# The opening of an attention and token-mixer block: c loaded as eight rows and spread by selector products, the gate's load moved behind the weights

## The chip, the cores and the metric

The kernel runs on one core of one Trainium2 chip. The metric is the device time of one execution in microseconds; lower is better. Of the core's engines, PE (TensorE) multiplies, DVE (VectorE), ACT (ScalarE) and POOL (GpSimd) work on elements, and SP (SyncE) issues the transfers. Each engine runs its own instructions strictly in order and waits on semaphores for the others.

## The reference, cut to what matters

The block takes x of 2048 tokens by 1024 channels and a condition c of 1024 numbers. Its first half is an attention over four segments of 512 tokens with a memory between the segments; its second half mixes tokens with a two-layer network.

```python
mod = (_silu(c) @ w_mod).reshape(c.shape[0], 6, 1, -1)
sa, ca, ga, sb, cb, gb = (mod[:, 0], mod[:, 1], mod[:, 2], mod[:, 3], mod[:, 4], mod[:, 5])
h = _layernorm(x, axis=-1) * (1 + ca) + sa
x = x + ga * _A_ref(h, A_wq, A_wk, A_wv, A_wo, A_beta)
...
g = _sigmoid(beta).reshape(1, H, 1, 1)
o = g * a_mem + (1.0 - g) * a_dot
```

So every element of h needs two modulation vectors, sa and ca, and these need silu(c) times a 1024 by 2048 part of w_mod. The gate g, one number for each of 32 heads, weighs the memory against the attention.

## The kernel before, in words

Nothing may start on PE before h exists. The opening therefore does the following.

- The 4 KB vector c is loaded as csb, 128 partitions by 8 (line 98). ACT and DVE make silu(c) from it (lines 99 to 103); DVE copies it out to bc, 128 by 8 by 128 (line 262); PE transposes bc in eight pieces (line 266) and ACT copies the result to scb (line 267): now every partition holds all 1024 values.
- Four tiles of x (128 tokens by 1024) are loaded (line 198). DVE takes their statistics (BN_STATS and BN_AGGR, lines 212 and 213, and a few short instructions on mvs, lines 217 to 220), ACT normalises them (line 222).
- For each of eight chunks of 128 channels two tiles wm of w_mod are loaded (line 284). DVE multiplies each by scb and sums along the row into one column of saca (line 285); line 288 adds 1.
- PE transposes a chunk of the four x tiles (hps, line 227), ACT evicts it with scale and bias from saca (line 229), and the result is split into a high and a low half (lines 113 and 116) as a page h. Weights are loaded raw (rawv, rawq, line 144) and split in the same way into wv and wq.
- PE then projects: nps are keys and values (line 182), qps queries (line 190), for heads of group 0 and group 1. A projection takes high by high first and then the products with the low halves, which DVE or POOL make.
- Segment 1 follows with x tiles 4 to 7 in the same way.

The gate is loaded by one transfer that reads beta for all 128 partitions (line 300), made on ACT and DVE (lines 301 to 304), and multiplied on POOL into bdg, one pair of instructions for each of eight groups (lines 318 and 321). bdg is first needed where DVE multiplies the first memory update up into MZ (line 429), the gate itself by the first values product (line 505).

In the attention, sx, sy and sz (line 445) are scores for the row maxima, which DVE reduces (line 446); a (lines 469 to 476) are scores again, whose exponentials p ACT writes, POOL selects (line 480) and splits into ph (line 484), which PE multiplies by the values (pv, line 498).

No engine's order is written by hand. A planner (class Order) records the program, gives each instruction a modelled duration and runs it forward and backward a few times; set_order then fixes the order of PE, DVE, ACT, POOL and SP. A load whose source is read again for every partition (a partition step of 0) is modelled with an added latency, DMA_SPREAD, of 7000 ns. The planner sees the whole program, so a change of the opening may change the order everywhere behind it.

Of the kernel before, what the change touches and what calls it, by code (L numbers as in the profile page):

```python
# [9 lines left out]
F32 = mybir.dt.float32  # L10
# [4 lines left out]
ALU = mybir.AluOpType  # L15
# [29 lines left out]
def attention_and_mlp(ctx, tc, x, wq, wkv, wo, beta, w1, b1, w2, b2, c, wm_a, wm_b, out):  # L45
# [25 lines left out]
    top = top_pool.__enter__()  # L71
    edge.tile([P, 8], F32, name="pad")
    acst.tile([P, 8], F32, name="pad2")
    psum = ctx.enter_context(tc.tile_pool(name="psum", bufs=1, space=PSUM))
# [22 lines left out]
    csb = acst.tile([P, 2, NK], F32, name="csb")  # L97
    SY.dma_start(csb[:, 0], c)
    A.activation(csb[:, 1], csb[:, 0], AF.Exp, scale=-1.0)
    V.tensor_scalar_add(csb[:, 1], csb[:, 1], 1.0)  # L100
    V.reciprocal(csb[:, 1], csb[:, 1])
    sc = const.tile([P, NK], F32, name="sc")
    V.tensor_mul(sc, csb[:, 0], csb[:, 1])

    saca = acst.tile([P, NK, 2], F32, name="saca")
# [154 lines left out]
    xs = {0: [load_x(s1p, tt) for tt in range(4)]}  # L260
    bc = s1p.tile([P, NK, P], F32, name="bc")
    V.tensor_copy(bc, sc.unsqueeze(2).to_broadcast([P, NK, P]))
    for i in range(2):
        ps = bank("pj", 2, f"scps{i}")
        for j in range(4):
            T.transpose(ps[:, 128 * j:128 * j + 128], bc[:, 4 * i + j], ident)
        A.copy(scb[:, 512 * i:512 * i + 512], ps)
# [25 lines left out]
    for g in range(2):  # L293
        first_chunk(g, NK - 1)
    xs[1] = [load_x(s2p, tt) for tt in range(4, 8)]
    norm_tiles(s2p, xs[1])
    for ct in range(NK):
        h_chunk(s2p, xs[1], 1, ct)
    gate = top.tile([P, 3, H], F32, name="gate")
# [4 lines left out]
    V.tensor_scalar(gate[:, 1], gate[:, 0], -1.0, 1.0, op0=ALU.mult, op1=ALU.add)  # L304

    left.__exit__(None, None, None)
# [651 lines left out]
HOLD = 1000.0  # L958
EARLY = 60000.0
STAY = 3000.0  # L960
SLACK = 1.06
# [17 lines left out]
def size_of(a):  # L979
    return math.prod(s[1] for s in a.ap) * mybir.dt.size(a.dtype)  # L980
# [51 lines left out]
def cost(x):  # L1032
# [20 lines left out]
    if e == "DVE":  # L1053
        if op == "ISA":
            return 135 + 1.05 * n, 220 + 1.05 * n, False
        if op == "TensorTensor":
            d = 145 + 1.055 * n
        elif op == "TensorScalarPtr":
            d = 190 if n < 64 else 120 + 1.1 * n
        else:  # L1060
            d = {"TensorCopy": 820, "BNStats": 680, "TensorReduce": 554}.get(op, 195)
# [16 lines left out]
class Order:  # L1078
# [155 lines left out]
    def side(x):  # L1234
# [26 lines left out]
    def forward(self, key):  # L1261
        n, E = len(self.X), self.E
        key = [-1e18 if i in self.follows else k for i, k in enumerate(key)]
        strong, weak, open_ = [[] for _ in range(n)], [[] for _ in range(n)], [0] * n
# [7 lines left out]
        ready, start, fin, seq = [0.0] * n, [0.0] * n, [0.0] * n, []  # L1272
        free, heap, future, link = defaultdict(float), defaultdict(list), defaultdict(list), 0.0
        last, port = "", 0.0
# [8 lines left out]
        def add(i):  # L1283
# [23 lines left out]
        while len(seq) < n:  # L1307
            t, e, i = self.pick(free, heap, future, key)
            x = self.X[i]
            if x.opcode == "DMACopy" and size_of(x.outs[0]) > BULK and link - t - ISSUED > BACKLOG:  # L1310
# [33 lines left out]
            if x.opcode == "DMACopy":  # L1344
                held, takes, more = transfer(x)
                if takes:
                    link = max(link, t + held + ISSUED) + takes
# [123 lines left out]
```

## Time and profile before

| | us |
|---|---|
| median of three runs | 2205.39 |
| lowest and highest of the three | 2204.5 and 2207.26 |
| the profiled execution | 2210.61 |
| its span, first to last instruction | 2208.9 |
| PE busy in it | 2162.7 (98%) |
| DVE busy | 1732.7 (78%) |
| ACT busy | 1097.1 (50%) |
| POOL busy | 725.7 (33%) |

All times inside the execution count from the first instruction. A row of the timeline gives the start, the duration, the engine, the line, the operation, what it writes and reads, and in brackets how long the engine stood idle before it and what ended that. In the windows, each engine's busy time is followed by the number of instructions in parentheses.

### The profile page before, as it was taken

How to read it: one execution, taken by the hardware profiler on the slowest of the kernel's cores; microseconds unless marked ns; L12 is line 12 of the kernel's file. 1: busy time of each engine (PE TensorE's matmuls, PEld its weight loads, DVE VectorE, ACT ScalarE, POOL GpSimd, SP SyncE). 2: the span in 40 equal slices, each digit the busy share in tenths (PEclk: the TensorE clock that was granted, in tenths of full speed). 3: DMA queues.
4: the chain of work that ended last, by engine and by line, in shares of the span. 5: the costliest groups of instructions: out<-in, count | busy, mean ns of one | idle time of the engine just before them, and what ended most of it. 6: DMA issues, size and time to landing. Idle time of an engine off the chain costs nothing.

```text
span 2208.9 us, 38272 instructions
## 1 busy us (share of the span) xinstructions
PE 2162.7 (98%) x13738; PEld 1876.5 (85%) x13738; DVE 1732.7 (78%) x3818; ACT 1097.1 (50%) x2008; POOL 725.7 (33%) x827
## 2 busy tenths in 40 slices
PE   6999999999999999989999999999999999999999
PEld 6899998989988999878878888888888888888887
DVE  8777777867787756678997555898889787878787
ACT  5688787566666665653443333633334242424232
POOL 3376676476777755551001000043321000000000
PEclk9999999999999999999999999999999999999999
DMA  9666676796777644664467555775549241414134
GB/s 370 189 204 189 192 223 196 244 288 201 224 213 235 181 135 107 191 211 157 139 238 277 191 194 197 276 278 200 201 175 337 86 157 58 149 53 148 58 124 152
DMA packets 174897, 421.74 MB, mean 191 GB/s; under 512 B 17492, under 2 KB 71796, under 8 KB 165748
## 3 DMA queue, kind: packets, MB, share of 16 engines
q1 hardware_dynamic: 174708, 419.30, 57.9%
q8 instruction: 109, 1.79, 0.3%
q14 instruction: 80, 0.66, 0.1%
HBM read 242.00 MB, written 126.37 MB: 167 GB/s over the span
## 4 chain that ended last, share of the span: by engine, by line
PE 83%; DVE 7%; POOL 2%; DMA 2%; ACT 2%; issue 1%; SPq 0%; DVEq 0%; POOLq 0%; ACTq 0%
PE mx L787 46%; PE nps L182 13%; PE qps L190 6%; PE po L688 4%; PE pv L498 4%; POOL ph L484 2%; PE a L469 1%; PE sz L445 1%; PE sx L445 1%; PE rd L417 1%; PE up L427 1%; PE a L472 1%; PE a L475 1%; PE sy L445 1%; PE ops L513 1%
## 5 line engine op out<-in xcount | busy, mean ns | idle before, releaser
L787 PE MATMUL mx<-bU,sp 128*128 128x512 f32 x2352 | 533.7, 389 | 0.9 <-DVE bU L116 0.9
L787 PEld LDWEIGHTS mx<-bU,sp 128*128 128x128 f32 x2352 | 441.3, 188 | 93.2 <-DVE bU L116 1.3
L113 ACT CAST sp<-wr 128x384 fp32r<-128x384 f32 (+2 forms) x408 | 218.4, 545 | 474.3 <-PE mx L787 386.8
L182 PE MATMUL nps<-wv,h 128*128 128x256 f32 x3072 | 444.8, 284 | 0.8 <-POOL h L116 0.6
L787 PE MATMUL mx<-bA,sp 128*128 128x512 f32 x1764 | 433.5, 389 | 1.6 <-ACT cc L792 0.7
L484 POOL TENSOR_TENSOR ph<-p,ph 128x640 f16<-128x640 f32 x256 | 385.3, 1524 | 110.1 <-ACT ph L482 109.0
L182 PEld LDWEIGHTS nps<-wv,h 128*128 128x128 f32 x3072 | 405.6, 189 | 7.0 <-POOL h L116 0.8
L787 PEld LDWEIGHTS mx<-bA,sp 128*128 128x128 f32 x1764 | 330.4, 188 | 72.7 <-ACT cc L792 1.3
L116 DVE TENSOR_TENSOR sp<-wr,sp 128x384 fp32r<-128x384 f32 (+2 forms) x408 | 260.4, 646 | 60.6 <-ACT sp L113 60.1
L794 DVE TENSOR_TENSOR ac<-mx,ac 128x512 f32<-128x512 f32 x280 | 190.7, 688 | 94.6 <-PE mx L787 93.4
L190 PE MATMUL qps<-h,wq 128*128 128x512 f32 x768 | 198.7, 400 | 0.1
L482 ACT CAST ph<-p 128x1280 f16<-128x1280 f32 x128 | 161.4, 1261 | 52.5 <-POOL p L480 51.5
L688 PE MATMUL po<-wo,ots 128*128 128x512 f32 x768 | 182.4, 392 | 0.5 <-ACT mv L125 0.5
L480 POOL TENSOR_SCALAR_AFFINE_SELECT p<-p 128x256 f32<-128x256 f32 x256 | 117.6, 469 | 188.8 <-ACT p L477 94.8
L688 PEld LDWEIGHTS po<-wo,ots 128*128 128x128 f32 x768 | 143.6, 189 | 29.8 <-ACT mv L125 0.9
L190 PEld LDWEIGHTS qps<-h,wq 128*128 128x128 f32 x768 | 140.8, 190 | 29.7 <-PE sz L445 0.5
L787 PE MATMUL mx<-bB,sp 128*128 128x512 f32 x588 | 165.9, 389 | 0.0
L446 DVE CUSTOM_DVE_ANT_0 sx<-sx,mask 128x128 f32<-128x128 f32 (+1 forms) x256 | 110.9, 434 | 69.6 <-PE sx L445 68.9
L659 POOL TENSOR_TENSOR tu<-cc 128x512 f32<-128x512 f32 x14 | 19.1, 1364 | 399.5 <-DVE cc L923 372.1
L787 PEld LDWEIGHTS mx<-bB,sp 128*128 128x128 f32 x588 | 110.4, 188 | 23.0
L498 PE MATMUL pv<-vp,ph 128*128 128x97 bf16 (+1 forms) x2560 | 117.1, 200 | 1.7 <-DVE am L505 1.0
L794 DVE TENSOR_TENSOR cc<-mx,cc 128x512 f32<-128x512 f32 x140 | 95.2, 684 | 25.6 <-PE mx L787 22.0
(179 smaller groups left out, 3258.3 us busy)
## 6 DMA issues: line engine op xcount, KB each, us to landing
sk<-sg SPq DMA_DIRECT2D x384, 128.0 KB
wr<-in_w_dram SPq DMA_DIRECT2D x28, 1024.0 KB
wr<-in_w_dram SPq DMA_DIRECT2D x32, 768.0 KB
bstu<-ucd SPq DMA_DIRECT2D x28, 768.0 KB
wv<-wsp SPq DMA_DIRECT2D x36, 512.0 KB
wsp<-wv SPq DMA_DIRECT2D x32, 512.0 KB
rawm<-in_wm_b_dram SPq DMA_DIRECT2D x32, 512.0 KB
pcd<-cc SPq DMA_DIRECT2D x14, 1024.0 KB
```

The lines of the kernel that those rows point to most:

```text
L113: A.copy(hi, src)
L116: lo_eng.tensor_tensor(lo, src, hi.bitcast(F32), op=ALU.subtract)
L182: T.matmul(ps[:, aa], h[:, j, 128 * tt:128 * tt + 128], wt[:, i, o:o + 256], start=(n == 0), stop=(n >= 6 * NK - 2), skip_group_check=True)
L190: T.matmul(ps, wt[:, i, o:o + 128], h[:, j], start=(k + n == 0), stop=(3 * k + n == 3 * NK - 1))
L446: V.tensor_tensor_reduce(o, o, mask[:, 384 - 128 * i:], 1.0, -3.0e38, op0=ALU.add, op1=ALU.max, accum_out=mx[:, h % 2, i:i + 1])
L480: G.affine_select(w, w, pattern=[[0, 2], [1, 128]], compare_op=ALU.is_ge, fill=0.0, base=0, channel_multiplier=-1)
L482: A.copy(ph[:, 0], p32)
L484: G.tensor_tensor(ph[:, 1, c], p32[:, c], ph[:, 0, c], op=ALU.subtract)
L498: T.matmul(pv[:, i, 0:w], ph[:, part, o:o + 128], d["vp"][:, j, h, 0:w], start=(n == 0), stop=(n == 19), skip_group_check=True)
L688: T.matmul(ps, os_[:, i, P * ct:P * ct + P], wop[ct, nh][:, j], start=(n == 0), stop=(n == 3 * NK - 1))
L787: T.matmul(ps, ops[q][:, i, P * k:P * k + P], b[:, j], start=(m == 0 and first), stop=(m == 3 * nk - 1), skip_group_check=True)
L794: V.tensor_tensor(d, ps, d, op=ALU.add)
```

## The change: what it does

- c is loaded as cr, 8 partitions by 128. silu is made there, on 8 partitions. POOL writes a selector sel of 8 by 8 by 128 that is 1 in row k for block k and 0 elsewhere; PE multiplies each block of sel with cr, which puts row k of cr on all 128 partitions. The copy bc and the transposes go.
- The code of the gate moves ahead of segment 1's loads in the program, but the planner holds a load that reads one row for every partition back to 45000 ns of its own clock (SPREAD), and puts a load of at most 4 KB that waits for nothing first (small).
- In the first 30000 ns of the planner's clock, DVE and ACT may idle up to 250 and 100 ns for an instruction that is more urgent by over 200 (WAIT, EAGER). One duration of short DVE instructions in the planner's costs goes from 190 to 155.
- Two numbers, LINK0 and QUICK, are added with values that change nothing. A pad of 8 columns is allocated in the place of the removed tile sc.

```diff
+    const.tile([P, 8], F32, name="pad1")
...
     csb = acst.tile([P, 2, NK], F32, name="csb")
-    SY.dma_start(csb[:, 0], c)
-    A.activation(csb[:, 1], csb[:, 0], AF.Exp, scale=-1.0)
-    V.tensor_scalar_add(csb[:, 1], csb[:, 1], 1.0)
-    V.reciprocal(csb[:, 1], csb[:, 1])
-    sc = const.tile([P, NK], F32, name="sc")
-    V.tensor_mul(sc, csb[:, 0], csb[:, 1])
...
-    bc = s1p.tile([P, NK, P], F32, name="bc")
-    V.tensor_copy(bc, sc.unsqueeze(2).to_broadcast([P, NK, P]))
+    sel = s1p.tile([NK, NK, P], F32, name="sel")
+    G.memset(sel, 1.0)
+    G.affine_select(sel, sel, pattern=[[-1, NK], [0, P]], compare_op=ALU.is_equal, fill=0.0, base=0, channel_multiplier=1)
+    cr = s1p.tile([NK, 2, P], F32, name="cr")
+    SY.dma_start(cr[:, 0], c)
+    A.activation(cr[:, 1], cr[:, 0], AF.Exp, scale=-1.0)
+    V.tensor_scalar_add(cr[:, 1], cr[:, 1], 1.0)
+    V.reciprocal(cr[:, 1], cr[:, 1])
+    V.tensor_mul(cr[:, 0], cr[:, 0], cr[:, 1])
     for i in range(2):
         ps = bank("pj", 2, f"scps{i}")
         for j in range(4):
-            T.transpose(ps[:, 128 * j:128 * j + 128], bc[:, 4 * i + j], ident)
+            T.matmul(ps[:, 128 * j:128 * j + 128], sel[:, 4 * i + j], cr[:, 0], start=True, stop=True)
         A.copy(scb[:, 512 * i:512 * i + 512], ps)
...
-    xs[1] = [load_x(s2p, tt) for tt in range(4, 8)]
-    norm_tiles(s2p, xs[1])
-    for ct in range(NK):
-        h_chunk(s2p, xs[1], 1, ct)
     gate = top.tile([P, 3, H], F32, name="gate")
     SY.dma_start(gate[:, 0], bass.AP(tensor=beta.tensor, offset=beta.offset, ap=[[0, P], [1, H]]))
...
+    xs[1] = [load_x(s2p, tt) for tt in range(4, 8)]
+    norm_tiles(s2p, xs[1])
+    for ct in range(NK):
+        h_chunk(s2p, xs[1], 1, ct)
...
+LINK0, SPREAD, QUICK = 0.0, 45000.0, 1.0
+EAGER = 200.0
+WD, WA = 250.0, 100.0
+SOON = 30000.0
+WAIT = {"DVE": WD, "Activation": WA}
...
-            d = 190 if n < 64 else 120 + 1.1 * n
+            d = 155 if n < 64 else 120 + 1.1 * n
...
+    def small(self, i):
+
+        x = self.X[i]
+        return x.opcode == "DMACopy" and not self.needs[i] and size_of(x.outs[0]) <= 4096
+
+    def spread(self, i):
+
+        x = self.X[i]
+        return x.opcode == "DMACopy" and not self.needs[i] and x.ins[0].ap[0][0] == 0
...
-        key = [-1e18 if i in self.follows else k for i, k in enumerate(key)]
+        key = [-1e18 if i in self.follows else -1e17 if self.small(i) else k for i, k in enumerate(key)]
...
+            if self.spread(i):
+                more = max(0.0, SPREAD - ready[i])
...
+            soon = WAIT.get(e, 0.0) if t < SOON else 0.0
+            if soon and future[e] and future[e][0][0] <= t + soon:
+                near = [(key[j], r, j) for r, j in future[e] if r <= t + soon]
+                k, r, j = min(near)
+                if k < key[i] - EAGER and r < t + self.C[i][0]:
+                    heapq.heappush(heap[e], (key[i], i))
+                    free[e] = r
+                    continue
...
-        "c": f("c").reshape(NK, P).T,
+        "c": f("c").reshape(NK, P),
```

What this does to the engines' order shows at three places. The line numbers are those of each kernel. First, SP's issues from the start of the program, before and then changed; x, csb, cr, gate, rawv, rawq and wm are the tiles that the transfers fill.

```order
L198 DMA x_134<-in_x_dram 128x1024
L98 DMA csb<-in_c_dram 128x8
L198 DMA x_136<-in_x_dram 128x1024
L300 DMA gate<-in_beta_dram 128x32
L198 DMA x_138<-in_x_dram 128x1024
L198 DMA x_140<-in_x_dram 128x1024
L144 DMA rawv_0_202<-in_wkv_dram 128x1024
L284 DMA wm_0_196<-in_wm_a_dram 128x1024
```

```order
L259 DMA cr<-in_c_dram 8x128
L192 DMA x_129<-in_x_dram 128x1024
L192 DMA x_131<-in_x_dram 128x1024
L192 DMA x_133<-in_x_dram 128x1024
L192 DMA x_135<-in_x_dram 128x1024
L138 DMA rawv_0_204<-in_wkv_dram 128x1024
L285 DMA wm_0_198<-in_wm_a_dram 128x1024
```

c's transfer went from second to first place, and the gate's, which stood fourth, now stands 33rd, behind the last wm and the first store of split weights. Second, ACT up to the first cast of a chunk of h, from the cast of group 0's rawq on, before and then changed.

```order
L113 CAST wq_0_0_0_212<-rawq_0_210 128x512
L113 CAST wq_0_0_1_215<-rawq_0_210 128x512
L222 ACTIVATE x_138<-x_138,mvs 128x1024
L222 ACTIVATE x_140<-x_140,mvs 128x1024
L229 ACTIVATE h_0_0_224<-hps_0_219,saca 128x512
L113 CAST h_0_226<-h_0_0_224 128x512
```

```order
L107 CAST wq_0_0_0_214<-rawq_0_212 128x512
L107 CAST wq_0_0_1_217<-rawq_0_212 128x512
L216 ACTIVATE x_133<-x_133,mvs 128x1024
L216 ACTIVATE x_135<-x_135,mvs 128x1024
L107 CAST wv_1_0_0_239<-rawv_0_237 128x512
L223 ACTIVATE h_0_0_226<-hps_0_221,saca 128x512
L223 ACTIVATE h_0_1_259<-hps_1_254,saca 128x512
L107 CAST h_0_228<-h_0_0_226 128x512
```

A cast of group 1's first raw weights and the eviction of a second chunk now stand ahead of the first cast of h. Third, DVE around the low half of h's fifth chunk (h_4), before and then changed; x_620 to x_626 and x_628 to x_634 are the x tiles of segment 1.

```order
L285 SCALAR_TENSOR_TENSOR wm_0_449,saca<-wm_0_449,scb 128x1024
L285 SCALAR_TENSOR_TENSOR wm_1_452,saca<-wm_1_452,scb 128x1024
L116 TENSOR_TENSOR h_4_416<-h_0_4_414,h_4_416 128x512
L288 TENSOR_SCALAR saca<-saca 128x1
L285 SCALAR_TENSOR_TENSOR wm_0_496,saca<-wm_0_496,scb 128x1024
```

```order
L286 SCALAR_TENSOR_TENSOR wm_0_498,saca<-wm_0_498,scb 128x1024
L206 BN_STATS st<-x_628 128x6
L206 BN_STATS st<-x_630 128x6
L206 BN_STATS st<-x_628 128x6
L206 BN_STATS st<-x_630 128x6
L206 BN_STATS st<-x_632 128x6 x2
L206 BN_STATS st<-x_634 128x6 x2
L289 TENSOR_SCALAR saca<-saca 128x1
L207 BN_AGGR mvs<-st 128x2 x4
L110 TENSOR_TENSOR h_4_418<-h_0_4_416,h_4_418 128x512
```

The statistics of all four x tiles of segment 1 moved ahead of h_4's low half, together with two more products of wm.

On POOL, the eight pairs that make bdg stood ahead of the fill of v and of segment 1's h, and now stand behind them, directly ahead of the first select of p.

More of the change, by code (lines that the diff above doesn't have):

```diff
@@ L1272, in forward @@
         ready, start, fin, seq = [0.0] * n, [0.0] * n, [0.0] * n, []
-        free, heap, future, link = defaultdict(float), defaultdict(list), defaultdict(list), 0.0
+        free, heap, future, link = defaultdict(float), defaultdict(list), defaultdict(list), LINK0
         last, port = "", 0.0
@@ L1345, in forward @@
                 held, takes, more = transfer(x)
+                if t < EARLY:
+                    takes *= QUICK
                 if takes:
```

## The prediction

> **What bounds the kernel now.** I read the busy times of seven stretches first, which I set by the program's stages.
>
> ```profile
> 0.00:22.50 22.50, 5.45 (x20) 3.48 (x21) 15.85 (x42) 11.80 (x19) 2.47 (x19) 1.00 0.87 332
> 22.50:28.40 5.90, 5.90 (x27) 5.37 (x26) 5.90 (x12) 5.71 (x10) 5.42 (x8) 1.00 1.03 410
> 28.40:64.60 36.20, 36.20 (x271) 33.99 (x269) 31.21 (x66) 20.50 (x36) 15.43 (x23) 1.00 0.92 336
> 64.60:72.00 7.40, 6.77 (x59) 6.57 (x57) 7.04 (x14) 6.58 (x15) 4.69 (x4) 1.00 0.97 323
> 72.00:100.00 28.00, 26.42 (x188) 23.52 (x189) 21.74 (x80) 14.99 (x31) 8.11 (x11) 1.00 0.60 182
> 100.00:980.00 880.00, 860.40 (x7756) 795.33 (x7755) 645.26 (x1947) 595.82 (x1094) 586.92 (x697) 1.00 0.67 201
> 980.00:2209.00 1229.00, 1221.55 (x5431) 1008.27 (x5429) 1005.67 (x1664) 441.70 (x807) 102.69 (x69) 1.00 0.50 175
> ```
>
> The columns are the stretch in us, its length, then PE, PEld, DVE, ACT and POOL busy, the granted clock, the DMA share and GB/s. PE is idle 17.05 us before 22.5, not at all from 22.5 to 64.6, 0.63 + 1.58 = 2.2 us from there to 100, 19.6 us in the rest of the attention and 7.45 us in the remainder. The change can therefore act in three ways: start PE's dense work earlier, remove part of the 2.2 us, or move part of the 19.6 us. Nothing else of the 2208.9 us is open to it.
>
> What holds the start is the loads. The DMA in four stretches of 5 us:
>
> ```profile
> 0.00:5.00 5.00, 0.00 (x0) 0.00 (x0) 0.17 (x1) 1.49 (x2) 2.47 (x19) 1.00 0.58 196
> 5.00:10.00 5.00, 1.94 (x8) 1.57 (x8) 3.82 (x9) 1.68 (x4) 0.00 (x0) 1.00 0.78 265
> 10.00:15.00 5.00, 0.00 (x0) 0.00 (x0) 4.36 (x12) 1.91 (x5) 0.00 (x0) 1.00 1.03 419
> ```
>
> From 10 us on the queue runs full: a 512 KB load takes 0.524 MB / 419 GB/s = 1.25 us. Between 5 and 10 us it moved (419 - 265) x 5 = 0.77 MB less than that, 1.84 us of full rate. The issues ahead and ACT's order behind them show what waits:
>
> ```profile
> 0.81 0.39 SPq L198 DMA_DIRECT2D x<-in_x_dram  x1
> 1.25 0.42 SPq L98 DMA_DIRECT2D csb<-in_c_dram  x1
> 2.19 0.43 SPq L300 DMA_DIRECT2D gate<-in_beta_dram  x1
> ...
> 10.57 1.29 DVE L212 BATCH_NORM_STATS2 st<-x 128x6 f32<-128x512 f32 x2 [1.58 <-DMA x<-in_x_dram]
> ...
> 4.58 0.21 ACT L99 ACTIVATE csb<-csb 128x8 f32<-128x8 f32 x1 [2.50 <-DMA csb<-in_c_dram]
> 13.09 0.62 ACT L113 CAST wv<-rawv 128x512 fp32r<-128x512 f32 x1 [3.47 <-DMA rawv<-in_wkv_dram]
> 14.43 2.36 ACT L222 ACTIVATE x<-x,mvs 128x1024 f32<-128x1024 f32 x2
> 16.93 1.14 ACT L113 CAST wq<-rawq 128x512 fp32r<-128x512 f32 x2
> 17.97 2.37 ACT L222 ACTIVATE x<-x,mvs 128x1024 f32<-128x1024 f32 x2
> 20.91 0.78 ACT L229 ACTIVATE h<-hps,saca 128x512 f32<-128x512 f32 x1 [0.57 <-PE hps L227]
> 21.72 0.62 ACT L113 CAST h<-h 128x512 fp32r<-128x512 f32 x1
> ```
>
> ACT sits 3.47 us until the first raw weights land at 13.09. Its normalisations, evictions and the cast of h's first chunk follow in that order, and PE's first projection starts at 22.51 behind the cast. The third x, which DVE waits for, landed at 10.57, and rawv two loads later at 13.09: 1.26 us each, so the shortfall is over by then and lay in front of the third x. There stand the gate's load (beta, one row read for all 128 partitions) and c's (128 rows of 32 bytes).
>
> **The change part by part.**
>
> *Loads.* c now goes first, as eight rows; the gate's load goes behind the weights; the four x then follow without a gap. Upper end of the gain: the issue of c (0.42 at 1.25, and csb arrives 3.3 us after its issue, of which one x load ahead of it is 1.25) gives about 2.1 us from issue to use, so x's first bytes follow c's at about 1.25, and the third x lands at 1.25 + 2.1 + 3 x 1.25 = 7.1, 3.5 us before. Lower end: if the shortfall is the queue's own ramp and stays, only the issue slots move: two slots leave (0.42 + 0.43), one comes ahead (0.42), 0.43 us. I take 3.0 us, the shortfall of 1.84 in that stretch and more of the poor 196 GB/s before it; rawv lands at 10.1, rawq three loads on at 13.85, group 1's rawv at 17.6.
>
> *ACT to the first projection.* In the new order ACT casts rawq from 14.0 to 15.2 (1.14 as before), normalises two x to 17.6 (2.37), then casts one half of group 1's raw weights (0.62, landed at 17.6) and evicts two chunks of h (2 x 0.78) before the first cast of h (0.62): 17.6 + 0.62 + 1.56 + 0.62 = 20.4. Before, it evicted one chunk and waited 0.57. So of 3.0 us, 2.0 arrive: the first projection starts at 20.45 instead of 22.51. With the lower end, 0.43, the extra cast and eviction make it 0.5 to 0.7 us later than before. DVE's two products for chunk 0, priced below at 1.15 each, are done by 14.7, before the evictions at 18.2 ask for them.
>
> *Selector products.* Eight products of 8 partitions replace one DVE copy and eight transposes, and POOL writes the selector first. The nearest rows:
>
> ```profile
> 1.04 0.53 POOL L84 MEMSET mask<- 128x512 bf16 x1
> 1.60 0.30 POOL L82 TENSOR_SCALAR_AFFINE_SELECT ident<-ident 128x128 f32<-128x128 f32 x1
> ...
> 6.30 1.94 PE L266 MATMUL scps<-ident,bc 128*128 128x128 f32 x8 [6.30 <-DVE bc L262]
> ```
>
> The new selector has 1,024 elements in a row: between the two rows as they stand (0.83) and twice the fill with eight times the select (3.5), so it is ready between 1.7 and 4.4. The new products may take 1.94, as the old did from 6.30, to twice that, and end between 5 and 8.3. It is first needed by DVE at about 11.9. Cover of more than 3 us: cost 0.
>
> *Does DVE keep up?* PE is the bound after its start only while h arrives. The new DVE order puts eight BN_STATS of segment 1 ahead of h's fifth chunk (h_4). I add what DVE does from the first low half of h (20.4) to that of h_4.
>
> ```profile
> 17.78 1.29 DVE L116 TENSOR_TENSOR wq<-rawq,wq 128x512 fp32r<-128x512 f32 x2
> 20.12 1.22 DVE L285 SCALAR_TENSOR_TENSOR wm<-wm,scb 128x1024 f32<-128x1024 f32 x1
> 21.27 1.22 DVE L285 SCALAR_TENSOR_TENSOR wm<-wm,scb 128x1024 f32<-128x1024 f32 x1
> 43.10 1.87 DVE L212 BATCH_NORM_STATS2 st<-x 128x6 f32<-128x512 f32 x3
> ```
>
> And PE's pieces, from the chain of waits (start, us, what):
>
> ```profile
> 23.50 1.11 PE hps L227 x4
> 28.41 1.37 PE nps L182 x12
> 29.78 0.69 PE qps L190 x3
> 38.46 0.44 PE hps L227 x4
> ```
>
> The columns are start and duration. Ten wm products at 1.15 (20.12 to 21.27), eight low halves at 0.62 (1.29 for two), eight BN_STATS at 0.62 (1.87 for three), 0.9 of small work: 11.5 + 5.0 + 5.0 + 0.9 = 22.4, so h_4 stands at 42.8. PE gets there after eight chunks of two groups at 1.37 + 0.69 = 2.06 (16.5 us), four sets of transposes at 0.44, 0.1 for a rest, 1.4 us of h_4's high half, and a slow start: from 22.51 to 28.41 it took 5.9 us for 2.06 + 2 x 0.44 = 2.94, four transposes costing 1.11 where later 0.44. That is 2.96 us lost, which I keep. 20.45 + 16.5 + 1.76 + 0.1 + 1.4 + 2.96 = 43.2. DVE is 0.4 us ahead: no stall, with a margin that an error of 2% removes.
>
> The clock column reads 1.00 through that slow start. [...]
>
> *The seam at 64.6 to 100.* Before, ACT came to segment 1's last three x so late:
>
> ```profile
> 55.39 3.56 ACT L222 ACTIVATE x<-x,mvs 128x1024 f32<-128x1024 f32 x3
> ```
>
> Now they follow the last cast of h, at about 48 (DVE's 42.8, then the rest of its list up to chunk 7). I credit 1.0 of the 2.2 us idle, with 0 and 2.2 as ends.
>
> *The gate.* Its work on POOL moves from a time when POOL had nothing else to behind the h halves of segment 1.
>
> ```profile
> L318 POOL TENSOR_TENSOR bdg<-bd,gate 128x128 f32<-128x128 f32 x8 | 8.3, 1036 | 19.5 <-DVE gate L303 19.5
> L321 POOL COPY bdg<-bd 128x4 f32<-128x4 f32 x8 | 7.3, 915 | 0.0
> ...
> 74.41 0.12 POOL L354 MEMSET v<- 128x16 f32 x1 [2.55 <-PE nps L182]
> 87.20 0.41 POOL L480 TENSOR_SCALAR_AFFINE_SELECT p<-p 128x256 f32<-128x256 f32 x1 [12.68 <-ACT p L477]
> 91.17 1.42 POOL L484 TENSOR_TENSOR ph<-p,ph 128x640 f16<-128x640 f32 x1 [2.99 <-ACT ph L482]
> ```
>
> 8.3 + 7.3 = 15.6 us now go into a gap of 12.68, behind the fill of v that waits for PE's second up product. With everything 3 us earlier that is 71.5 + 15.6 = 87.1, and the select of p is wanted at 84.2: 2.9 us late. POOL then waited 2.99 us for ACT, which covers it: cost 0 here, up to 4 if the pairs run as slowly as beside DVE's wm products. The load itself stands behind the last wm, so its shortfall of 1.84 us falls on stores of split weights, which nobody awaits.
>
> *The rest of the order.* All engines' orders differ throughout the attention. Its idle time has these parts:
>
> ```profile
> PE a L475 <- ACT p L470: 7.2, 13, 1.3
> PE a L469 <- DMA sk<-nt: 4.6, 3, 2.9
> ```
>
> Both repeat over many iterations and may fall out better or worse: 0 taken, 4 us either way (a fifth of 19.6) as ends.
>
> *Sum:* -2.0 (start) - 1.0 (seam) + 0 (selector, DVE, gate) + 0 (order) = -3.0 us. The profiled execution took 2210.61 (span 2208.9), 5.2 over the median 2205.39 and 3.4 over the slowest of the three, so I carry the difference and not the level: 2207.6 there, **2202.4** by the median. I call within 0.2% (4.4 us) no change; this forecast lies within it.
>
> **The rivals.**
>
> *The new order is also the better one.* The shifted start plus 2 to 6 us of the 19.6 idle: 2196.5 to 2200.5. For it: 13 waits on ACT's p of up to 1.3 us, which an order that lets an engine wait a little for the more urgent instruction may shorten. Against: that allowance holds only in the first 30 us of the planner's clock, so later parts change without aim.
>
> *Given back at h_4.* If PE leaves its slow start sooner, or DVE runs later, PE waits for DVE behind the eight BN_STATS: every microsecond of it takes one of the gain. For: a margin of 0.4 us. Against: the gate's products no longer run on POOL beside them. Or the DMA shortfall stays, and the extra cast costs 0.6 us. Either way 2203.5 to 2207.
>
> *POOL late (slower).* The gate's pairs reach beyond the cover of 2.99 us. The point is 87.2: at 1.95 us a pair they end there; at 2.5 us they end at 71.5 + 20 = 91.5, 4.3 us past the cover, and PE's first values product stands still for as long, since its order is fixed; POOL, busy 587 of 880 us afterwards, hands on part of it. 4.3 + 2 for the next heads - 2.0 for the start = +4.3, and beyond with an order that falls out worse: 2208 to 2212. For: DVE's maxima run densely there. Against: the 15.6 us were measured beside DVE's long wm products already.
>
> **How the numbers follow.** Forecast (-1 to -5) 0.42, of which 0.08 is beyond -4.4; better order 0.30; given back 0.11, of which 0.02 beyond +4.4; POOL late 0.17. Faster: 0.30 + 0.08 = 0.38; slower: 0.17 + 0.02 = 0.19; same: 0.43. The range of 2196.5 to 2210.0 leaves out the ends of the second and the last case; the forecast's own is 2200.4 to 2204.4.
>
> **What would show it.** ACT's first cast of rawv at about 10.1 and PE's first projection at about 20.5 bear out the load and ACT steps; a cast at 12 or later says that the gate was not the cause. An idle PE ahead of a projection at about 43 with DVE as its releaser shows h_4. The gap ahead of POOL's first select of p, and whether PE waits for ph, settle the gate. PE's idle time from 100 to 980 against 19.6 settles the order. I am wrong if the start comes 2 us earlier and the end does not, with no new idle time up to 100: then the reordered attention decided.

## The result and the profile after

| kernel | median, us | lowest to highest | runs |
|---|---|---|---|
| before | 2207.26 | 2204.5 to 2209.39 | 7 |
| changed | 2213.71 | 2211.92 to 2216.76 | 7 |

The changed kernel is slower: ratio 1.0031, 95% interval 1.0022 to 1.0041, where 2202.4 and a gain were forecast. A later repeat gave 2212.3 against 2208.26, ratio 1.0019 (1.0007 to 1.0031).

The windows of the changed kernel, in the prediction's stretches (columns as there):

```profile
0.00:22.50 22.50, 9.58 (x39) 7.75 (x40) 18.05 (x42) 14.83 (x24) 4.37 (x21) 1.00 0.90 356
22.50:28.40 5.90, 5.90 (x39) 5.55 (x39) 5.87 (x12) 2.52 (x5) 0.00 (x0) 1.00 1.03 409
28.40:64.60 36.20, 36.20 (x271) 34.02 (x270) 32.33 (x68) 24.16 (x41) 9.13 (x15) 1.00 0.99 352
64.60:72.00 7.40, 7.40 (x64) 7.32 (x64) 7.40 (x20) 3.58 (x11) 1.87 (x4) 1.00 0.95 344
72.00:100.00 28.00, 25.50 (x176) 22.55 (x175) 19.97 (x79) 17.18 (x35) 12.20 (x26) 0.94 0.54 147
100.00:980.00 880.00, 857.72 (x7727) 792.77 (x7726) 637.92 (x1931) 593.59 (x1083) 584.77 (x692) 0.99 0.67 200
```

PE's idle time is the length less PE's busy time. Up to 22.5 us it fell from 17.05 to 12.92, and the seam at 64.6 to 72 closed. From 72 to 100 it rose from 1.58 to 2.50, from 100 to 980 from 19.60 to 22.28. And the granted clock, 1.00 in these rows before, now reads 0.94 and 0.99.

The opening itself came as forecast. In the timeline and the windows of the changed kernel the first cast of raw weights starts at 10.23 (10.1 forecast, 13.09 before), PE's first projection at 20.81 (20.45 forecast, 22.51 before), and the DMA moves 400 GB/s between 5 and 10 us (265 before):

```profile
5.00:10.00 5.00, 3.37 (x16) 3.07 (x15) 5.00 (x10) 1.68 (x4) 0.29 (x4) 1.00 1.02 400
...
10.23 1.14 ACT L107 CAST wv<-rawv 128x512 fp32r<-128x512 f32 x2 [0.68 <-DMA rawv<-in_wkv_dram]
...
20.81 2.48 PE L176 MATMUL nps<-wv,h 128*128 128x256 f32 x10
```

What was lost later stands in the timeline as long waits of PE. Before had one over 1.8 us in its attention; the changed kernel has these four, and two more of 1.84 and 2.29 us at 942.0 and 963.5:

```profile
81.44 0.47 PE L469 MATMUL a<-sk 98*128 98x512 f32 x1 [2.06 <-DMA sk<-nt]
129.95 0.58 PE L475 MATMUL a<-sk 98*128 98x256 f32 x1 [1.91 <-ACT p L470]
380.51 0.47 PE L469 MATMUL a<-sk 98*128 98x512 f32 x1 [3.25 <-DMA sk<-nt]
596.29 0.39 PE L475 MATMUL a<-sk 98*128 98x256 f32 x1 [2.87 <-ACT p L470]
```

The second cost hides in the clock column. The record of the granted clock drops to a half four times in the changed kernel's attention, each time for 3.4 us, and windows laid on these stretches show it:

```profile
82.20:85.60 3.40, 3.40 (x11) 2.61 (x11) 1.42 (x5) 2.20 (x5) 0.41 (x1) 0.50 0.95 374
129.90:133.40 3.50, 3.45 (x29) 3.45 (x30) 1.99 (x6) 3.50 (x8) 0.81 (x2) 0.51 0.91 222
597.60:601.00 3.40, 3.40 (x15) 3.21 (x15) 1.89 (x7) 2.42 (x4) 1.64 (x4) 0.50 1.02 222
942.30:945.70 3.40, 3.40 (x28) 2.84 (x27) 1.33 (x6) 0.30 (x2) 2.75 (x2) 0.50 0.89 201
```

PE counts as busy in them. In the first, query products in a row start 0.43 us apart, against 0.23 at the middle of those from 86 to 129 us. If PE does half the work there, each costs up to 1.7 us (an estimate: half of 3.4) that no idle time shows. Three of the four begin within 1.4 us of the end of a long wait of the rows above, the fourth 0.3 us behind the wait of 1.84 at 942.0. The profile of before has two such stretches:

```profile
464.90:468.30 3.40, 3.31 (x12) 3.02 (x13) 1.95 (x8) 3.01 (x5) 2.31 (x2) 0.50 1.03 410
946.20:949.60 3.40, 3.38 (x9) 2.82 (x10) 1.83 (x3) 0.45 (x1) 3.30 (x3) 0.50 0.86 340
```

### The profile page after: what moved, and what is told of

It is laid out like the page before. It is cut to its first block, busy times and chain, and to the rows that moved or that the text cites. A ratio compares the mean times of both kernels' runs of the same rounds, so it can differ in the third digit from the quotient of the medians.

```text
span 2210.2 us, 38274 instructions
## 1 busy us (share of the span) xinstructions
PE 2166.9 (98%) x13746; PEld 1880.9 (85%) x13746; DVE 1727.9 (78%) x3817; ACT 1101.1 (50%) x2008; POOL 717.9 (32%) x829
## 4 chain that ended last, share of the span: by engine, by line
PE 90%; DVE 4%; DMA 2%; ACT 2%; POOL 2%; issue 1%; SPq 0%; DVEq 0%; ACTq 0%; POOLq 0%
PE mx L787 48%; PE nps L176 14%; PE qps L184 7%; PE po L688 7%; PE pv L498 4%; PE sx L445 1%; PE a L469 1%; PE sz L445 1%; POOL ph L484 1%; PE up L427 1%; PE rd L417 1%; PE a L472 1%; PE a L475 1%; DMA rawv<-in_wkv_dram 1%; PE sy L445 1%
## 5 line engine op out<-in xcount | busy, mean ns | idle before, releaser
L498 PEld LDWEIGHTS <-ph 128*128 128x128 f16 x2560 | 108.2, 98 | 6.1 <-issue 1.5
```

Source lines behind the costliest of these rows:

```text
L498: T.matmul(pv[:, i, 0:w], ph[:, part, o:o + 128], d["vp"][:, j, h, 0:w], start=(n == 0), stop=(n == 19), skip_group_check=True)
```

## The experiments

The change has three parts that can be had singly: c first with its selector; the planner's two rules for the opening (the gate's load held back by SPREAD, the idling by WAIT); and the planner's number for short DVE instructions, 190 to 155. Behind the first third of the attention (from 310 us on) the orders of DVE, ACT, POOL and SP in the traces differ only with that number: with 190 all have the order of before there, with 155 all that of the changed kernel. The runs below were made in several sessions; before took 2207.26 to 2208.26 in them. Medians, with that of before in the same session:

| kernel | number | us | before | ratio (95%) |
|---|---|---|---|---|
| c first, no rules | 190 | 2206.12 | 2207.96 | 0.9993 (0.9984 to 1.0002) |
| c first, idling, load not held | 190 | 2205.89 | 2208.02 | 0.9991 (0.9981 to 1.0000) |
| c first, idling, load held | 190 | 2207.40 | 2207.96 | 0.9999 (0.9990 to 1.0007) |
| before with the number alone | 155 | 2220.49 | 2207.96 | 1.0051 (1.0035 to 1.0067) |
| c first, idling, load not held | 155 | 2207.12 | 2207.96 | 0.9994 (0.9985 to 1.0003) |
| the whole change | 155 | 2213.71 | 2207.26 | 1.0031 (1.0022 to 1.0041) |

**The number put back.**

```diff
-            d = 155 if n < 64 else 120 + 1.1 * n
+            d = 190 if n < 64 else 120 + 1.1 * n
```

> The changed kernel with one number put back: the planner's cost of short DVE instructions is 190 again, not 155. Its orders then equal those of the kernel before in the last four fifths of the program and keep the new opening. Theory 1 (the opening is worth about 4 us, and the attention's new order, which comes from the 155 alone, loses it and more): PE's first projection at 20.5 to 21.0 as in the changed kernel, PE idle at most 20 us from 100 to 980, at most two half-clock windows behind the opening, and 3 to 5 us under the kernel before, 2202 to 2204. Theory 2 (the loss comes from the opening's own instructions or loads, or from the gate's later work): still 3 to 7 us over the kernel before.

2207.40: the loss of some 6 us is gone, as expected, but not the 3 to 5 us under before that the opening should then have left. No half clock came, and PE is idle for 20.75 us from 100 to 980 (19.6 in before). Idle time came at new places at 63 to 75:

```profile
62.99 0.66 PE L221 MATMUL hps<-ident,x 128*128 128x128 f32 x4 [1.08 <-ACT h L223]
...
69.85 0.44 PE L445 MATMUL sx<-sk 96*128 96x384 f32 x1 [1.33 <-DVE mx L446]
...
74.92 0.83 PE L176 MATMUL nps<-wv,h 128*128 128x256 f32 x5 [0.87 <-DVE sg L110]
```

**Before with the number alone.** The same line, in the kernel before.

> The kernel before with that one number changed to 155 and nothing else. Its orders equal those of the changed kernel behind the first fifth. Theory 1: the attention's order alone loses 6.5 us plus the 4 us that the opening had gained: 9 to 11 us over the kernel before, 2216 to 2218, with stalls of 2 to 3 us at the places where the changed kernel has them (near 380, 596, 942 and 963 us). Theory 2: within 2 us of the kernel before.

2220.49, 12.5 us over before where 9 to 11 were expected. The opening is the old one, so the number alone loses time, and more than in the changed kernel. Its waits at 381.32 (3.30 us, for sk<-nt) and 603.49 (2.52 us, for p) are those of the changed kernel at 380.51 and 596.29.

**The load not held back, 155 kept.**

```diff
-LINK0, SPREAD, QUICK = 0.0, 45000.0, 1.0
+LINK0, SPREAD, QUICK = 0.0, 0.0, 1.0
```

> The changed kernel with the gate's load no longer held back (the hold is 0), so that it stands among the first loads again. Theory A (the gate's load, one row read for 128 partitions, made the DMA's shortfall of 1.84 us between 5 and 10 us): the windows from 5 to 10 us show 250 to 300 GB/s again instead of 400, ACT's first cast of raw weights comes at 12 to 13 us instead of 10.2, and PE's first projection 2 us later. Theory B (the shortfall came from c's 128 rows of 32 bytes or from the queue's ramp): the windows stay near 400 GB/s and the cast at 10.2 to 10.8. The end, by theory 1 on the attention's order, which is that of the changed kernel: by A 0 to 4 us over the changed kernel.

2207.12, 6.6 us under the changed kernel, where 0 to 4 over it were expected. Of the two theories on the start neither came out whole: from 5 to 10 us the DMA moves 360 GB/s, the first cast is at 11.52 (10.23 with the load held), the first projection at 22.35 (20.81). It has the changed kernel's later order, waits of 4.06 and 2.01 us at the same instructions included, but none from 72 to 100:

```profile
72.00:100.00 28.00, 27.99 (x225) 25.70 (x223) 22.57 (x87) 18.71 (x38) 9.68 (x13) 1.00 0.67 177
```

So the parts do not add: 155 costs 12.5 us with the old opening, about 1 with the new one and the load free, 6 with it held.

**c alone.** As above, and in addition

```diff
-WAIT = {"DVE": WD, "Activation": WA}
+WAIT = {}
...
-            d = 155 if n < 64 else 120 + 1.1 * n
+            d = 190 if n < 64 else 120 + 1.1 * n
```

> c loaded first as eight rows and spread by selector products, with the planner otherwise as in the kernel before: the gate not held, no idling, cost 190; the attention's order is that of the kernel before. Theory 1 with theory A: the gate's load still makes the shortfall, so the gain of the opening is small, and the time is 0 to 2 us under the kernel before. If c's 32-byte rows were the cause of the shortfall (theory B), the first projection starts 2 us earlier and the time is 2 to 4 us under it.

2206.12, 1.8 under before. The first cast is at 11.73, not at 10.23, and the first projection at 21.15. From 5 to 10 us the DMA moves 347 GB/s, half way between before and the changed kernel, but over the first 10 us together it moves no more than in before (230), where the whole change moves 286. So the eight rows alone do not lift the shortfall of the DMA; the held gate does:

```profile
0.00:10.00 10.00, 3.75 (x16) 3.48 (x16) 5.26 (x11) 3.22 (x6) 4.38 (x21) 1.00 0.68 232
...
11.73 0.62 ACT L107 CAST wv<-rawv 128x512 fp32r<-128x512 f32 x1 [1.68 <-DMA rawv<-in_wkv_dram]
```

**Two moves in the changed kernel's order.** Behind the planner, single instructions are moved on their engine.

```diff
+MOVES = [("PE", 445, 447, 452), ("Activation", 151, 152, 150)]
...
+    rows = defaultdict(list)
+    for i in seq:
+        rows[o.E[i]].append(i)
+    for e, a, b, c in MOVES:
+        part = rows[e][a:b]
+        rows[e][min(a, c):max(b, c)] = part + rows[e][c:a] if c < a else rows[e][b:c] + part
...
-    for i in seq:
+    for i in (i for r in rows.values() for i in r):
```

These rows of the changed kernel's timeline are the reason for the second move. At 122.5 POOL begins three ph products (5.06 us). DVE's low halves of weights beside them take 1.94 and 1.90 us, where those that meet no ph product take 0.69 at the middle; they delay the low half of sg, and with it ACT's rq; p stands behind rq, and PE's a behind p:

```profile
122.49 5.06 POOL L484 TENSOR_TENSOR ph<-p,ph 128x640 f16<-128x640 f32 x3
...
122.51 1.94 DVE L110 TENSOR_TENSOR wv<-rawv,wv 128x512 fp32r<-128x512 f32 x1
126.20 1.90 DVE L110 TENSOR_TENSOR wq<-rawq,wq 128x512 fp32r<-128x512 f32 x1
128.01 0.68 DVE L110 TENSOR_TENSOR sg<-qps,sg 128x512 fp32r<-128x512 f32 x1
...
128.73 0.60 ACT L388 ACTIVATE rq<-qps 128x512 f32<-128x512 f32 x1 [2.95 <-DVE sg L110]
129.22 0.68 ACT L470 ACTIVATE p<-a,shift 128x512 f32<-128x512 f32 x1
```

> The changed kernel with two places of its order altered and nothing else: on PE the first pair of score products a for the first head goes behind one sx and four query products, which had stood behind it (it waited 2.06 us at 81.4 for the transfer sk<-nt); on ACT the exponentials p of the head at 129 go ahead of the evicted query rq, which had waited 2.95 us for DVE. Theory (the order puts an instruction directly behind a wait while other work stands ready behind it, and each such stall is followed by a stretch of 3.4 us at a granted clock of 0.5, worth 1.7 us): both stalls and both stretches go, 2.06 + 1.7 + 1.91 + 1.7 = 7.4 us, about 2206 by the median and 2204 to 2205 in the profile, with no stretch of half clock before 500 us. Rival (the stalls only show where another engine is late, and the next instruction waits instead): idle time turns up within 5 us of each place and the time stays within 2 us of the changed kernel's 2213.7.

2209.84, 3.9 and 2.5 us under the two measurements of the changed kernel: a third to a half of what was expected, and against the measurement of the same session (ratios to before 1.0006 and 1.0019) the two intervals overlap. In its timeline the first wait is 0.53, the second went to another instruction and is 0.58; but the later two stayed:

```profile
82.24 0.47 PE L469 MATMUL a<-sk 98*128 98x512 f32 x1 [0.53 <-DMA sk<-nt]
129.10 0.72 PE L417 MATMUL rd<-MZ,pq 128*128 128x132 f32 x4 [0.58 <-DVE pq L391]
376.65 0.47 PE L469 MATMUL a<-sk 98*128 98x512 f32 x1 [3.11 <-DMA sk<-nt]
593.53 0.58 PE L475 MATMUL a<-sk 98*128 98x256 f32 x1 [2.58 <-ACT p L470]
...
593.40:600.20 6.80, 6.67 (x42) 6.48 (x43) 3.23 (x11) 4.38 (x8) 2.83 (x5) 0.50 1.00 246
```

No half clock came before 500, as forecast, but at 593 it lasted 6.8 us instead of 3.4. The waits are the order's, and behind the two that were shortened the half clock went with them; but the time did not fall by the 7.4 us that two waits and two stretches of 1.7 us would make, and another wait drew a longer stretch than before. The last section shows which waits drew one.

**Three waits attacked where the load is not held.** To the 2207.12 kernel, with the code of the two moves,

```diff
+MOVES = [("SP", 358, 362, 356), ("PE", 2992, 2993, 3002), ("Activation", 771, 772, 770),
+         ("PE", 7906, 7907, 7913), ("PE", 7909, 7910, 7913)]
```

In the timeline of the kernel that it starts from, the four small transfers of nt stand on SP behind a 512 KB store and a 512 KB load; their issues take 3.77 us, and PE waits for them:

```profile
366.05 0.39 SPq L159 DMA_DIRECT2D wsp<-wq  x1
366.54 0.38 SPq L138 DMA_DIRECT2D rawv<-in_wkv_dram  x1
367.01 3.77 SPq L459 DMA_DIRECT2D sk<-nt  x4
...
373.41 0.47 PE L469 MATMUL a<-sk 98*128 98x512 f32 x1 [4.06 <-DMA sk<-nt]
590.29 0.39 PE L475 MATMUL a<-sk 98*128 98x256 f32 x1 [2.01 <-ACT p L470]
946.99 0.52 PE L469 MATMUL a<-sk 98*128 98x512 f32 x1 [1.74 <-DMA sk<-nt]
```

> The changed kernel with the gate's load not held back (2207.1), and its three longest stalls attacked in the order: the four transfers of nt at 367 go ahead of a store and a load of weights on SP and their score product a goes behind ten other instructions on PE (stall 4.06 at 373.4); p goes ahead of rq on ACT at 589 (stall 2.01 at 590.3); a goes behind po products at 947 (stall 1.74). Theory (stalls of the order, with stretches of half clock behind two of them): 4.06 + 1.7 + 2.01 + 1.74 + 1.7 = 11.2 at most, of which I expect 7 to 10: 2197 to 2200, under both kernels. Rival (the wait moves on to the next instruction): 2205 to 2207.

2198.76 (2195.56 to 2199.93), ratio to before 0.9958 (0.9946 to 0.9971): 9.5 us under before and faster than both kernels. In its timeline the four issues now take 2.69 us, and PE does not wait at that a, nor at the third place; the second wait went to another a and is shorter, and one of 2.34 us came behind the third:

```profile
365.81 2.69 SPq L459 DMA_DIRECT2D sk<-nt  x4
...
370.33 0.48 PE L469 MATMUL a<-sk 98*128 98x512 f32 x1
...
586.08 0.50 PE L469 MATMUL a<-sk 98*128 98x512 f32 x1 [1.33 <-ACT p L473]
949.54 0.47 PE L469 MATMUL a<-sk 98*128 98x512 f32 x1 [2.34 <-DMA sk<-nt]
...
100.00:980.00 880.00, 863.91 (x7776) 797.59 (x7773) 643.81 (x1955) 599.30 (x1095) 592.93 (x702) 1.00 0.68 202
```

PE is idle 16.1 us from 100 to 980, where the kernel it starts from has 21.4 and before 19.6, and half clock comes once (950.5) instead of twice. The five moves were made together; how much each of them gave is not shown.

**Both kernels once more.**

> The changed kernel once more. If its long stalls belong to the order, PE stands idle again over 1.5 us at the same instructions, the first score product (81.4), the third score product of the head at 130, and at 380 and 596, and the median is 2212 to 2215. If they were chance of one execution, they are elsewhere.

2212.30. The four waits came again, and a fifth of 1.83 us at 481.9 with them: chance of one execution is excluded as their cause. The two at 942.0 and 963.5 did not come again.

```profile
81.66 0.54 PE L469 MATMUL a<-sk 98*128 98x512 f32 x1 [1.76 <-DMA sk<-nt]
130.21 0.39 PE L475 MATMUL a<-sk 98*128 98x256 f32 x1 [1.95 <-ACT p L470]
378.92 0.76 PE L469 MATMUL a<-sk 98*128 98x512 f32 x1 [3.32 <-DMA sk<-nt]
598.32 0.38 PE L475 MATMUL a<-sk 98*128 98x256 f32 x1 [2.01 <-ACT p L470]
```

Half clock came only behind the first and the third of them (81.9 and 378.9): 1.76 us sufficed there, and 1.95 did not at 130.2. These are two windows of 3.41 us, as long as a stretch, one ahead of 81.92 and one that ends 14 such windows later:

```profile
78.50:81.92 3.42, 1.66 (x9) 1.06 (x8) 2.33 (x11) 1.49 (x4) 0.00 (x0) 1.00 0.51 153
126.30:129.71 3.41, 1.96 (x17) 1.75 (x15) 3.41 (x5) 0.73 (x2) 1.49 (x1) 1.00 0.55 220
```

The wait of 1.76 lies whole in the first, in which PE is busy for 49%; the wait of 1.95 ends 0.50 us behind the second, in which it is busy for 57%.

> The kernel before once more, for a second profile. Its first execution that was profiled took 2210.6 where the median is 2208. If the 2.9 us stall and half clock at 946 belong to the order, they come again; if they are chance, this profile has none there and ends about 3 us sooner. The opening should repeat: the first cast of raw weights at 13.1 and the first projection at 22.5, each within 0.5 us.

2204.92. The wait of 2.87 us at 946 did not come, as chance would have it, though half clock came once behind one of 1.75 at 933.2; but the opening did not repeat within 0.5 us:

```profile
11.60 0.62 ACT L113 CAST wv<-rawv 128x512 fp32r<-128x512 f32 x1 [2.02 <-DMA rawv<-in_wkv_dram]
...
21.01 0.99 PE L182 MATMUL nps<-wv,h 128*128 128x256 f32 x3
```

The first cast is at 11.60 instead of 13.09, the first projection at 21.01 instead of 22.51. The execution from which the prediction was made had an opening 1.5 us late.

**The gate's pairs on POOL put later.** With the number at 190, the pairs, which there stood between the low halves of h_4 and h_6 of segment 1, go behind them.

```diff
+MOVES = [("Pool", 33, 36, 29), ("Pool", 37, 38, 32), ("Pool", 42, 43, 33), ("Pool", 45, 46, 34)]
```

> The changed kernel with the cost of 190 (2207.4, whose order behind the first fifth is that of before), and with the gate's eight pairs on POOL put behind the low halves of h_4 and h_6 of segment 1, which they had stood between. With 190 PE stood idle 1.08 + 1.33 + 0.87 = 3.3 us between 62 and 76, against 0.63 + 0.38 = 1.0 in the second profile of before. Theory (the held gate's pairs lengthen DVE's casts and products beside them, 0.41 to 0.9 and 0.68 to 1.5 us, and so give back what the earlier start won): about 2 of the 3.3 us go, median 2205 to 2206. Rival (the start's gain only meets the next waits, whatever POOL does): idle time there stays over 2.5 us, median 2206.5 to 2208.

2207.47 (ratio to before 0.9996, 0.9987 to 1.0005): the theory fell. PE is idle 2.94 us at 63 to 75 instead of 3.28, in a wait of 1.08 at 63.0, as it was, and one of 1.86:

```profile
74.42 0.83 PE L176 MATMUL nps<-wv,h 128*128 128x256 f32 x5 [1.86 <-DVE sg L110]
```

The two shorter waits of 1.33 and 0.87 became one longer. With the load held and 190, the 1.5 us between 2205.89 and 2207.40 are within the intervals, and no run found what gives them back.

**Other values of the number.** The line with 155 is changed again, first to 172 and 140, with the load held.

> The changed kernel with the modelled duration of short DVE instructions at 172, half way between 155 and 190. Theory A (the number is a seed: any value gives another order of the whole attention, whose stalls fall out anew): 2203 to 2222, with long stalls of PE at other places than with 155, and no trend from 190 over 172 to 155. Theory B (a smaller number makes the orders worse): between 2207.4 and 2213.7.

> The changed kernel with that number at 140, below the 150 ns that the short DVE instructions take in the profile. Theory A (a seed): 2203 to 2222, with stalls at other places again. Theory B (smaller is worse): above 2214.

2209.34 (ratio 1.0008, 0.9998 to 1.0017) and 2218.09 (1.0048, 1.0031 to 1.0066). With 190 and 155 that made a trend, which was not what I held likely. So the trend was tested against chance, with 140 and 190 where the load is not held (SPREAD 0.0) and 225 where it is:

> The changed kernel with the gate's load not held back and the number at 140 (with 155 this took 2207.1). Theory A (the number only draws another order): 2203 to 2218, on either side of 2207.1. Theory B (smaller is worse, as 190, 172, 155 and 140 gave 2207.4, 2209.3, 2213.7 and 2218.1 with the load held): 2211 to 2214, the same 4.4 above the kernel with 155.

> The changed kernel with the gate's load not held back and the number at 190. Theory B: 6 us under 2207.1, so 2200 to 2202. Theory A: anywhere from 2203 to 2218; and if the order behind the opening is that of before, near the 2206.1 to 2207.4 that the two kernels with c first and 190 took.

> The changed kernel, the load held, the number at 225, above all that the profile shows of those instructions (209 ns for most, 162 for others). Theory B: at or under 2207. Theory A: 2203 to 2222, as likely above 2210 as under it.

The trend fell at 225 (2219.49, where it asked for 2207 or less), at 190 with the load free (2205.89, for 2200 to 2202) and at 140 with it free (2220.51, for 2211 to 2214). A third theory was left: that the order is best where the number is right. The 200 instructions that it stands for in seven groups of before take 142 to 210 ns by group, 195 on average (40 at 208 or 209 in each of three groups, 48 at 162; not 193, as the expectations below have it), and 190 was the best value so far. So values close to it on both sides were tried, and 225 once more.

> The changed kernel, the load held, the number at 200. Theory C (the order is best where the number is right: the 200 instructions that it stands for take 193 ns on average in the profile of before, and 190 came out best of 225, 190, 172, 155 and 140): 2206 to 2209. Theory A (chance): anywhere from 2205 to 2222, and since four of the five other draws with the load held lay at 2209 or above, likely above 2209.

> The changed kernel, the load held, the number at 182. Theory C: 2206 to 2209, between 2207.4 at 190 and 2209.3 at 172. Theory A: anywhere from 2205 to 2222.

> The changed kernel with the load not held back, the number at 225. Theory C: 2213 to 2220, as 225 gave 2219.5 with the load held. Theory A: anywhere from 2205 to 2222.

> The changed kernel with the load not held back, the number at 200. Theory C: 2204 to 2208, about the 2205.9 that 190 gave. Theory A: anywhere from 2205 to 2222.

All values, medians in us:

| load | 225 | 200 | 190 | 182 | 172 | 155 | 140 |
|---|---|---|---|---|---|---|---|
| held | 2219.49 | 2220.26 | 2207.40 | 2216.03 | 2209.34 | 2213.71 | 2218.09 |
| not held | 2218.97 | 2228.18 | 2205.89 | | | 2207.12 | 2220.51 |

The third theory fell clearly: 200 gave 2220.26 and 2228.18, the latter the slowest of all (ratio 1.0090, 1.0072 to 1.0109), and 182 gave 2216.03 (1.0030, 1.0020 to 1.0041). With the load free, 200 and 140 (2228.18 and 2220.51) also lie above what the expectations had given to chance (2222 and 2218): the spread was taken too small. What is left is that each value draws another order, and that the order of before, which 190 gives, is an uncommonly good one. Eleven kernels here have another (ten of the table and before with 155); from 255 to 490 us on these are six orders, since kernels with one value share it. They lie 1.2 to 22.3 us over the kernel with the same opening and 190, the middle one 12.1. How the 190 came to stand there is not to be seen in the runs.

## Why the prediction was wrong

**The failed step is "The rest of the order": 0 taken, 4 us either way.** The reordered attention decided, as the last paragraph of the prediction had named for this case, with two differences: new idle time came already at 72 to 100, and its price was above the bound. With 190 put back the kernel takes 2207.40, with 155 2213.71: the order of the 155 costs 6.3 us with this opening. The bound was a fifth of PE's idle time, and idle time is what the profile shows. The changed kernel's idle time from 72 to 980 rose by 0.92 + 2.68 = 3.6 us, inside that bound; but two more stretches of half clock than before came with it, counted as busy. So it was wrong, too, that only PE's idle time was open to the change. These rows show both, from the first values product (pv) to the last, of the changed kernel and then of the second profile of before:

```profile
93.48:1052.69 959.21, 936.93 (x8163) 859.37 (x8162) 706.46 (x2085) 625.85 (x1144) 601.73 (x708) 0.99 0.66 197
...
92.42:1044.92 952.50, 933.78 (x8171) 857.46 (x8170) 710.00 (x2088) 623.25 (x1146) 602.80 (x709) 1.00 0.66 199
```

They differ by 6.7 us: 3.6 of idle time, and 3.1 of busy time with three stretches of half clock instead of one. Ahead of them the changed kernel is 1.1 us late in spite of its earlier start, with one stretch of half clock there (82.2), and behind them it gains 0.8. Together this is 7.0, the difference of the two spans (2210.2 and 2203.2). How much of the busy time is half clock can only be estimated: in the twelve traces with 155 or 190, PE's busy time from the first pv to the last grows from 932.5 and 933.4 with no such stretch to 937.3 with four, about 1.2 us each by a line through all twelve.

The attention's order changed in two ways, and the prediction costed neither. Behind its first third it changed through one number that the change lists (with 190 put back, that part is the order of before); in the first third through that number and the opening's rules together. The runs showed that it takes both to lose the 6 us: 2207.40 with 190 put back, 2207.12 with the load let free, 2213.71 with both.

**Loads.** The cast at 10.23 bears out the 3.0 us against the profile used, and the gate as their cause, though up to half of the 3.0 was chance of that execution. The first cast lay at 11.60, 12.76 and 13.09 in three executions with the old loads, at 11.52 to 12.32 in seven with c first and the gate not held, and at 10.12 to 10.52 in ten with the gate held as well. By the middle values (12.76, 11.90 and 10.2) c's eight rows bring 0.9 to the cast and the held gate 1.7; only the second is clear of the scatter.

**ACT to the first projection.** Right within 0.4 us (20.81 for 20.45), partly by luck: the second profile of before has it at 21.01, only 0.2 later. PE's idle time up to 22.5 fell by 4.1 against the profile used and by 2.6 against the second, but 1.8 of that is only the selector products, which keep PE busy for longer than the transposes did. What PE gained shows further on: its 201st projection product (nps and qps) starts at 52.50, against 55.72 and 54.21 (at most 3.2 and 1.7 gained, since some other work of PE stands later in the new order). So the 2.0 was of the right size, but against the second profile not for its reason: PE left its slow start sooner. The first record of the granted clock lies at 24.13, against 27.98 and 26.42; the 1.00 of the clock column ahead of these times has no record behind it.

**Selector products** cost nothing that PE's chain met, as said: they took 3.75 us, the upper end, and ended at 8.37, and DVE's first wm product starts at 12.09.

**DVE and h_4.** No wait came: PE is busy for all of the 42.1 us from 22.5 to 64.6. This rival fell.

**The seam.** The 0.63 us at 64.6 to 72 went, but 72 to 100 became 0.92 worse; the credit of 1.0 was wrong, since the attention's first heads stand there, and with them the order.

**The gate's pairs on POOL.** The rival on the slow side had the right sign for the time and the wrong mechanism. The eight pairs took 5.1 us instead of 15.6, now that they ran where DVE has no long wm products (that this is the reason fits the 396 ns for 1036, but no run tests it alone):

```profile
L318 POOL TENSOR_TENSOR bdg<-bd,gate 128x128 f32<-128x128 f32 x8 | 3.2, 396 | 0.7 <-DVE gate L300 0.7
L321 POOL COPY bdg<-bd 128x4 f32<-128x4 f32 x8 | 1.9, 240 | 0.0
```

The first select of p waited 7 us for ACT behind them. POOL was early, not late.

**"The new order is also the better one"** had 0.30, a worse order no rival of its own. The argument against it, that parts beyond the first 30 us change without aim, should have turned it round: of the eleven redrawn orders nine were slower than before beyond their interval, none faster, and the two that were level (2209.34 and 2207.12) lay 1.9 and 1.2 us over the kernel with the same opening and 190.

## What to carry to other kernels

When a planner sets the order, a change of any of its numbers is a change of the whole order, and should be costed as a new draw on the far part, apart from what it does at its own place: from a good order the draw is mostly a loss, here up to 22 us where the opening could win 2. Most long waits belong to the order and come back at the same instructions (here four of six), so they can be listed from one profile, better two, and attacked by moving a waiting instruction behind ready work. Five moves gained 8.4 us here (2207.12 to 2198.76); two in the changed kernel gained 2.5 to 3.9. Before a gain of 2 us is worked out from an opening, a second profile of the same kernel shows whether it varies by as much.

## What the runs showed of the hardware

- **Half clock behind short waits.** Stretches of 3.4 us at a granted clock of 0.50 came behind waits of 1.32 to 4.06 us in the attention, not behind every one of that length, and eight times with no wait over 0.96 us in the 3.4 us ahead (once in before, at 464.9). In the record of the granted clock each of the six in the attention of before and of the changed kernel lasts 3413 ns, and the waits at five of them (1.84 to 2.87 us) were all shorter than that.
- **Which wait draws it.** Within each execution the stretches begin whole multiples of 3413 ns apart (14, 137 and 101 in the changed kernel), so its time can be cut into windows of that length at their beginnings. Cut so from 28 to 980 us, the 20 traces of this case have 21 windows in which PE was busy for less than 45%, and half clock follows every one of them; it follows 13 of the 26 windows with 45 to 56%, and of some 5530 above that only eight, all between 66 and 79%. So in these traces half clock went with how busy PE was in one such window, and not with the length of the wait alone: the changed kernel's wait of 1.91 us ends at 129.95, where a window ends too (44% busy), and half clock follows; its wait of 3.25 us at 380.5 falls across two (46 and 59%), and none does. What the eight others have in common is open.
- **DVE and POOL.** DVE's low half of weights, a difference of two operands in SBUF, took 1.94 us behind a ph product of POOL that had begun 0.02 us ahead of it; the 26 in the changed kernel that meet no ph product take 0.69 us at the middle. The low halves of sg, of which one operand lies in PSUM, take 0.67 to 0.69 beside ph products, too (22 of them). The 1.94 is 1.25 us more than the 0.69, and that ph product took 1.42. No run tests what makes the two kinds of low half differ.
- **Small transfers behind large ones.** Four issues of nt took 3.77 us directly behind a store and a load of 512 KB, 2.69 ahead of them, and 2.61 at the middle of the 51 places where the kernel with the load free issues four.
